# A 700-word memset on GpSimd in front of every indirect DMA, known to the schedule

## The chip, the core and the metric

The kernel runs on one core of a Trainium2 chip. What is measured is the device time of one execution in microseconds (us). The engines go by the names of the profile: PE is TensorE (PEld its weight loads), DVE is VectorE, ACT is ScalarE, POOL is GpSimd and SP is SyncE, which issues the plain DMAs. An *indirect* DMA (rows picked by a list of indices) is issued by POOL.

## The reference

A Fourier transform along the sequence, a complex linear layer with soft thresholding, the transform back, and then a mixture of 8 experts in which every expert takes exactly 2496 of the 19968 tokens, by a greedy assignment in the order of the logits:

```python
X = np.fft.rfft(x, axis=1)                       # x: 8 x 2496 x 256
Yr = Xr @ w_r - Xi @ w_i + b_r
Yi = Xr @ w_i + Xi @ w_r + b_i
Yr = np.sign(Yr) * np.maximum(np.abs(Yr) - lam, 0.0)   # Yi likewise
y = np.fft.irfft(Y, n=x.shape[1], axis=1)
...
logits = x @ w_gate                              # x = y as 19968 x 256, 8 experts
order = np.argsort(-flat)
for idx in order:                                # token, expert
    if assigned[tok] >= 0 or counts[e] >= cap: continue
    assigned[tok] = e; counts[e] += 1            # cap = 2496
...
for e in range(E):                               # w1[e]: 256 x 1024, w2[e]: 1024 x 256
    h = np.maximum(x[mask] @ w1[e], 0.0)
    out[mask] = h @ w2[e]
```

## The kernel before

The program has two parts that overlap a little. Up to about 640 us the transforms run as matrix products, batch by batch; in them POOL has elementwise work (L893 and L1116 write the low halves of numbers that are split in two for the matmuls). The transform's result goes to the DRAM tensor `YD`, one row of 256 words per token.

Then come the experts. Each has an *early* job of 512 tokens, whose lists are known before the last batches are transformed, and a *late* job of 1984 tokens, taken in an order that the routing decides. A late job of an expert consists of these steps, and each of the eight takes some 110 us:

- the router (DVE searches thresholds by counting, L419 and L423, with small matmuls L429 and L430; then a list of token numbers from matmuls L516, ACT's sign sums L521 and L522 and DVE),
- four gathers of the expert's weights by POOL (`Experts.load`, L578, buffers `raw`), split in two halves by ACT (L586) and DVE (L587),
- 16 gathers of 128 tokens each by POOL (L600), two into one buffer of the group `xg`,
- per chunk of 512 tokens (four gathers): eight transposes on PE (L615) into one PSUM bank (group `psx`, a single one), split by ACT (L618) and DVE (L619),
- the first layer on PE (L630), relu and split by ACT (L633) and DVE (L634),
- the second layer on PE (L646), 24 matmuls for 128 tokens, copied by ACT (L649) into one of the four buffers of the group `os` (in the profile xTh and xTl),
- 16 scatters of 128 tokens each by POOL (L653), each with a memset of a single word ahead of it (L652).

Names in the profile are those of the buffers, which the groups share: xg, xT and hid are names like yTl, s1st, z, FG and s2h.

No order is written out by hand. The class `Plan` takes all tasks with an engine, an assumed duration, a position and the tasks they depend on, simulates them, and at each step emits the task that can start first (the lowest position where several can). So the order of every engine's instructions follows from the assumed durations. An indirect DMA is such a task of POOL (`Kit.ind`, L309): 1.05 us of POOL, and a `load` that says when its data are there, by way of one queue for all DMAs:

```python
def ind(...): return self.plan.add('P', 1.05, pos, emit, reads, writes, load=moved(nbytes, run, 1.2, 1.4, late))
...
if t.load is not None:
    lead, work, back = t.load
    self.queue = max(self.queue, start + lead) + work
    t.end = self.queue + back
```

There are 352 indirect DMAs: 160 gathers and 160 scatters of tokens (32 of each in the early jobs) and 32 of weights. Once emitted, the order on an engine is fixed: each instruction waits for the semaphores of what it reads and for the instruction ahead of it.

Of the kernel before, what the change touches and what calls it, by code (L numbers as in the profile page):

```python
# [77 lines left out]
class Buf:  # L78

    def __init__(self, kind, alloc, state=False):  # L80
        self.state = state
        self.kind, self.alloc, self.t, self.got = kind, alloc, None, False
        self.writers, self.users = [], []
# [172 lines left out]
        return max(t.end for t in self.tasks)  # L256


LATE = dict(sp=2.0, raw=8.0, gather=2.0, scatter=3.0)
SLACK = dict(split=2.0, count=0.3, back=0.2, lists=0.5, os=0.3, hid=0.2)  # L260


def moved(nbytes, run, lead=1.6, back=1.8, late=0.0): return lead, nbytes / run * (0.009 + 3.68e-5 * run if run <= 4096 else 7e-5 * run) / 16, back + late
# [21 lines left out]
class Kit:  # L285
# [20 lines left out]

    def dma(self, pos, emit, nbytes, reads, writes, run=1024, late=0.0, **k): return self.plan.add('SP', 0.4, pos, emit, reads, writes, load=moved(nbytes, run, late=LATE['sp'] + late), **k)

    def ind(self, pos, emit, nbytes, reads, writes, run=1024, late=0.0): return self.plan.add('P', 1.05, pos, emit, reads, writes, load=moved(nbytes, run, 1.2, 1.4, late))  # L309


HALF = CAP / 2
# [242 lines left out]
class Experts:  # L555

    def __init__(self, K, H, YD, YDb, w1, w2, out):
        self.K, self.H, self.YD, self.YDb, self.out = K, H, YD, YDb, out
        self.w = (w1, w2)
        self.rows = (w1.rearrange("e d f -> (e d) f"), w2.rearrange("e (r m) d -> (e r) (m d)", m=4))  # L560
        self.spacer = K.one("spacer_b", [1, 1])
        self.scat = []

    def load(self, pos, e=None, wi=None):
# [3 lines left out]
        for k in range(2):  # L568
            for m in range(2):
# [7 lines left out]
                else:  # L577
                    K.ind(p, lambda r=r, k=k, m=m: K.P.indirect_dma_start(out=r.t, out_offset=None, in_=self.rows[k],  # L578
                                                                          in_offset=bass.IndirectOffsetOnAxis(ap=wi.t[:, m:m + 1], axis=0)), 524e3, [wi], [r], run=4096, late=LATE['raw'])

# [9 lines left out]
    def run(self, n, base, W, gi, go, gs, oi, oo, pos_g, early=False):  # L590

        K, H, plan, v = self.K, self.H, self.K.plan, self.K.v
        V, A, P, T = K.V, K.A, K.P, K.T
# [3 lines left out]
        for t in range(NT):  # L597
            if not t % 2: xg[t // 2] = K.sb("xg", [128, 2, 256])
            g = xg[t // 2]
            q = K.ind(pos_g(t), lambda t=t, g=g: P.indirect_dma_start(  # L600
                out=g.t[:, t % 2], out_offset=None, in_=self.YD[0:EB * S] if early else self.YD, in_offset=bass.IndirectOffsetOnAxis(ap=gi.t[:, go + t:go + t + 1], axis=0)),
                131e3, [gs[t]] + (self.YDb[0:EB] if early else self.YDb), [g], late=LATE['gather'])
            gi.users.append(q)
# [32 lines left out]
        def ffn2(c, q, pos):  # L636
            t = 4 * c + q
            M = min(128, n - 128 * t)
            ps, o = K.psum("pso", [128, 256]), K.sb("os", [128, 256])
            for qr in range(4):  # L640
                def mm(qr=qr):
                    k = 6 * qr
                    for ft in range(2 * qr, 2 * qr + 2):
                        hh, hl = hT[c, ft]
                        for a, w_ in ((hh, 0), (hh, 1), (hl, 0)):
                            T.matmul(ps.t[0:M], lhsT=a.t[:, 128 * q:128 * q + M], rhs=W2[ft // 4].t[:, w_, ft % 4], start=k == 0, stop=k == 23)  # L646
                            k += 1
                K.t(.708, pos + .5 * qr, mm, [W2[qr // 2]] + [x for ft in range(2 * qr, 2 * qr + 2) for x in hT[c, ft]], [ps], slack=SLACK['hid'])
            plan.add('A', .27, pos + 1, lambda: A.copy(o.t[0:M], ps.t[0:M]), [ps], [o], slack=SLACK['os'])  # L649

            def sc():
                P.memset(self.spacer.t, 0.0)  # L652
                ins = P.indirect_dma_start(out=self.out, out_offset=bass.IndirectOffsetOnAxis(ap=oi.t[0:M, oo + t:oo + t + 1], axis=0), in_=o.t[0:M], in_offset=None, bounds_check=N - 1, oob_is_err=False)  # L653
                for other in self.scat:
                    K.tc.declare_no_dep(ins.ins, other.ins, reason="distinct rows")
                self.scat.append(ins)
            K.ind(pos + 2, sc, 131e3, [o, oi], [], late=LATE['scatter'])

# [198 lines left out]
def phase_a(K, H, x, w_r, w_i, b_r, b_i, w_gate, cD1, cF, cG, cD5, YD, LG, NB=B):  # L857
# [25 lines left out]
    def add_dma(pos, emit, nbytes, reads=(), writes=(), eng='SP', after=(), run=1024):  # L883
        return plan.add(eng, 1.05 if eng == 'P' else 0.4, pos, emit, reads, writes, after=after, load=moved(nbytes, run, *((1.2, 1.4) if eng == 'P' else ()), late=LATE['sp']))

# [509 lines left out]
```

## Time and profile before

| | us |
|---|---|
| median of 3 runs (lowest to highest) | 1677.47 (1677.03 to 1680.85) |
| the profiled execution, whole | 1685.89 |
| its span, first to last instruction | 1684.0 |
| PE busy | 1569.3 (93%) |
| DVE busy | 1110.5 (66%) |
| ACT busy | 822.6 (49%) |
| POOL busy | 585.3 (35%) |
| mean granted clock of TensorE | 0.971 |

Times of the profile are microseconds from the span's start. A matmul's line gives the engine PE, the line of the kernel, the tile written and the tiles read. The granted clock is a share of TensorE's full speed: 1.00 is 2.4 GHz, 0.50 is 1.2 GHz. "Idle before" is the time in which the engine had nothing before that instruction, and behind the arrow stands what released it.

### The profile page before, as it was taken

The page shows a single profiled execution, that of the slowest core. Times are in us where ns is not written, and L with a number is a line of the kernel's source. Part 1 is how long each engine was busy: PE and PEld are TensorE (multiplying, and loading weights), DVE is VectorE, ACT ScalarE, POOL GpSimd, SP SyncE. Part 2 cuts the span into 40 slices and gives each one's busy share as a digit, 9 for nine tenths or more (in the row PEclk, how much of TensorE's full clock was granted, in tenths as well). Part 3 has the DMA queues.
Part 4 walks back from the last instruction along what each step waited for, and adds up shares of the span by engine and source line. Part 5 has one row for each costly group of instructions (what it writes and reads, how often), then busy time and mean ns, then how long its engine had stood idle before and what let it go on. Part 6 is the DMA issues. An engine that isn't in the chain of part 4 may idle for free.

```text
span 1684.0 us, 30703 instructions
## 1 busy us (share of the span) xinstructions
PE 1569.3 (93%) x10808; PEld 1379.7 (82%) x10808; DVE 1110.5 (66%) x3561; ACT 822.6 (49%) x1795; POOL 585.3 (35%) x711
## 2 busy tenths in 40 slices
PE   6999999999999989998998998997988989988997
PEld 3899999998888758986787887886878868867997
DVE  2666667668988855898788887785757645442321
ACT  1557767676687654445334343342433534542331
POOL 1014334343365553124326234233251242452121
PEclk7999999999999999999999999998999999989999
DMA  8777877877688554333112022121221111221000
GB/s 237 219 238 244 230 232 223 241 239 218 203 240 260 177 165 144 100 108 106 42 51 88 25 76 62 51 67 46 70 61 37 65 56 60 93 86 41 21 26 26
DMA packets 140071, 209.30 MB, mean 124 GB/s; under 512 B 31135, under 2 KB 102511, under 8 KB 139713
## 3 DMA queue, kind: packets, MB, share of 16 engines
q1 hardware_dynamic: 118612, 145.53, 28.8%
q0 software_dynamic: 21296, 61.73, 11.8%
q8 instruction: 87, 1.43, 0.4%
q14 instruction: 76, 0.62, 0.1%
HBM read 122.44 MB, written 84.75 MB: 123 GB/s over the span
## 4 chain that ended last, share of the span: by engine, by line
PE 68%; DVE 10%; issue 10%; ACT 3%; another core or an unknown queue 3%; POOL 3%; DMA 2%; SPq 0%; POOLq 0%; ACTq 0%; DVEq 0%
PE ps L646 19%; PE ps L630 12%; PE ps L1038 12%; PE p L630 6%; PE ps L1019 4%; PE ps L1052 4%; PE p L1086 3%; PE p L988 3%; POOL out_dram L653 2%; PE pt L1106 2%; PE ps L615 2%; DVE junk L419 1%; PE ps L1127 1%; DMA sh<-in_x_dram 1%
## 5 line engine op out<-in xcount | busy, mean ns | idle before, releaser
L1038 PE MATMUL ps<-wt,xTh 128*128 128x256 f32 x1280 | 245.5, 291 | 0.0
L1038 PEld LDWEIGHTS ps<-wt,xTh 128*128 128x128 f32 x1280 | 201.2, 190 | 5.4 <-issue 0.2
L1038 PE MATMUL ps<-wt,xTl 128*128 128x256 f32 x640 | 179.8, 281 | 0.7 <-DVE xTl L1029 0.7
L1116 POOL TENSOR_TENSOR yTl<-yr,yTh 128x468 bf16<-128x468 f32 (+1 forms) x88 | 97.9, 1113 | 173.4 <-ACT yTh L1113 128.9
L419 DVE SCALAR_TENSOR_TENSOR junk<-h_m,st,h_AG 128x156 bf16<-128x156 f32 (+1 forms) x472 | 155.4, 374 | 2.5
L653 POOL DMA_INDIRECT out_dram<-xTh,li x64 | 67.0, 1047 | 257.6 <-ACT xTh L649 244.3
L893 POOL TENSOR_TENSOR s2l<-s2c,s2h 120x512 fp32r<-120x512 f32 (+1 forms) x84 | 102.3, 1222 | 134.8 <-ACT s2h L890 131.3
L1038 PEld LDWEIGHTS ps<-wt,xTl 128*128 128x128 f32 x640 | 121.8, 190 | 0.9 <-DVE xTl L1029 0.9
L649 ACT COPY xTl<-ps 128x256 f32<-128x256 f32 x80 | 29.8, 373 | 169.5 <-PE ps L646 132.3
L649 ACT COPY xTh<-ps 128x256 f32<-128x256 f32 x80 | 29.9, 374 | 164.1 <-PE ps L646 122.3
L1019 PE MATMUL ps<-FG,sh 128*128 128x128 f32 x640 | 97.2, 283 | 7.3 <-DMA sh<-T 7.3
L1019 PEld LDWEIGHTS ps<-FG,sh 128*128 128x128 f32 x640 | 87.8, 194 | 15.8 <-issue 10.5
L653 POOL DMA_INDIRECT out_dram<-xTl,li x64 | 65.4, 1023 | 97.3 <-ACT xTl L649 82.6
L1029 DVE TENSOR_TENSOR xTl<-ps,xTh 128x512 fp32r<-128x512 f32 x80 | 54.9, 687 | 59.4 <-ACT xTh L1028 58.2
L1052 PE MATMUL ps<-z,FG 128*128 128x256 f32 x320 | 84.1, 385 | 3.4 <-DMA FG<-cG 1.1
L578 POOL DMA_INDIRECT xt<-in_moe_w_dram,wi x32 | 35.6, 1114 | 130.9 <-DVE h_certs L800 23.8
L1044 DVE TENSOR_TENSOR ps<-ps,bt 128x512 f32<-128x512 f32 x80 | 55.6, 694 | 32.4 <-PE ps L1038 29.3
L893 DVE TENSOR_TENSOR xl<-xt,xh 117x512 fp32r<-117x512 f32 (+1 forms) x77 | 61.6, 806 | 21.8 <-ACT xh L890 21.4
L1028 ACT CAST xTh<-ps 128x512 fp32r<-128x512 f32 x80 | 47.2, 590 | 49.4 <-PE ps L1019 43.8
L1111 DVE TENSOR_TENSOR yr<-pt,yTh 128x468 f32<-128x468 f32 (+1 forms) x77 | 48.1, 625 | 28.8 <-ACT yTh L1110 21.5
L646 PE MATMUL ps<-sh,yTh 128*128 128x256 f32 (+1 forms) x320 | 64.6, 284 | 2.4 <-ACT xTl L649 2.4
L1086 PE MATMUL p<-s2h,d 120*117 120x512 f32 (+1 forms) x168 | 66.6, 403 | 0.0
(722 smaller groups left out, 5097.8 us busy)
## 6 DMA issues: line engine op xcount, KB each, us to landing
sh<-T SPq DMA_DIRECT2D x40, 512.0 KB
T<-s4st SPq DMA_DIRECT2D x80, 256.0 KB
s2c<-T SPq DMA_DIRECT2D x80, 240.0 KB
YD<-yst SPq DMA_DIRECT2D x80, 234.0 KB
T<-s1st SPq DMA_DIRECT2D x73, 240.0 KB
xt<-in_moe_w_dram SPq DMA_DIRECT2D x32, 512.0 KB
xt<-in_x_dram SPq DMA_DIRECT2D x105, 156.0 KB
LG<-lgst SPq DMA_DIRECT2D x80, 21.9 KB
```

The lines of the kernel that those rows point to most:

```text
L419: v(cols + 59, p, lambda k=k: V.scalar_tensor_tensor(junk[k % 2].t[:, 0:cols], H.m[:, 0:cols], c.t[:, k // ng:k // ng + 1], ag(k % ng)[:, ...
L630: T.matmul(ps.t[:, 0:w], lhsT=W1[m].t[:, a, 128 * ft:128 * ft + 128], rhs=x_.t[:, 0:w], start=q + m == 0, stop=q + m == 3)
L646: T.matmul(ps.t[0:M], lhsT=a.t[:, 128 * q:128 * q + M], rhs=W2[ft // 4].t[:, w_, ft % 4], start=k == 0, stop=k == 23)
L649: plan.add('A', .27, pos + 1, lambda: A.copy(o.t[0:M], ps.t[0:M]), [ps], [o], slack=SLACK['os'])
L653: ins = P.indirect_dma_start(out=self.out, out_offset=bass.IndirectOffsetOnAxis(ap=oi.t[0:M, oo + t:oo + t + 1], axis=0), in_=o.t[0:M], in ...
L893: lambda: eng.tensor_tensor(lb[1](), src(), hb[1](), op=OP.subtract), [srcb, hb[0]], [lb[0]])
L1019: T.matmul(ps.t[:, i, 128 * dt:128 * dt + 128], lhsT=sh[k // 8].t[:, k % 8, 128 * dt:128 * dt + 128], rhs=at(Ft, k), start=True, stop=True)
L1038: T.matmul(ps3.t[:, i], lhsT=a.t[:, i, dt, o:o + 128], rhs=wt[c].t[:, w, dt], start=n == 0, stop=n == 11)
L1044: plan.add('V', dve(512), pos + 1.282, lambda ps3=ps3: V.tensor_tensor(ps3.t, ps3.t, bt[:, None, :].to_broadcast([128, 2, 256]), op=OP.add ...
L1052: T.matmul(ps4.t[:, i], lhsT=at(Gt, 2 * p + i), rhs=z.t[:, i], start=True, stop=True)
L1086: T.matmul(ps.t[0:M, gs_], lhsT=d5[0:k_, a, 0:M], rhs=v.t[0:k_, gs_], start=i == 0, stop=i == 2)
L1116: yq.append(plan.add('P', pool(2 * W), pos + 0.376, lambda yh=yh, yl=yl, yr=yr, W=W: P.tensor_tensor(yl.t[:, :, 0:W], yr.t[:, :, 0:W], yh. ...
```

## The change

Every indirect DMA is now issued right behind a memset of 700 words in one partition on POOL, into a buffer `gap` that nobody reads. The task in the plan gets longer by 0.982 us (0.1 + 1.26e-3 x 700), on POOL and in the lead of its data. The one-word memsets ahead of the scatters are gone.

```diff
+GAP = 700
...
-    def ind(self, pos, emit, nbytes, reads, writes, run=1024, late=0.0): return self.plan.add('P', 1.05, pos, emit, reads, writes, load=moved(nbytes, run, 1.2, 1.4, late))
+    def ind(self, pos, emit, nbytes, reads, writes, run=1024, late=0.0):
+        g = 0.1 + 1.26e-3 * GAP
+
+        def spaced():
+            self.P.memset(self.gap, 0.0)
+            return emit()
+        return self.plan.add('P', g + 1.05, pos, spaced, reads, writes, load=moved(nbytes, run, g + 1.2, 1.4, late))
...
-        self.spacer = K.one("spacer_b", [1, 1])
+        K.gap = K.one("gap", [1, GAP]).t
...
             def sc():
-                P.memset(self.spacer.t, 0.0)
                 ins = P.indirect_dma_start(out=self.out, ...
```

The memset has no operand in common with the DMA behind it, so it waits for nothing but POOL itself. Since the plan's durations change, so does the order on all engines; the same instructions are emitted otherwise. The lines of the new kernel are 6 or 7 higher (L600 is L607, L615 is L622, L630 is L637, L646 is L653, and the scatter L653 is L659; the memset is L314).

On POOL, at the late job of the fifth expert (the one whose gathers begin at 1229.62 us in the trace before): the tiles gathered are yTl, s1st, z, FG, s2h, two gathers each, and the scatters, from xTh and xTl, belong to the expert ahead of it. Before:

```order
467 L600 DMA yTl_16590<-YD,li_16584 128x256 x2
468 L600 DMA s1st_16621<-YD,li_16584 128x256 x2
469 L600 DMA z_16660<-YD,li_16584 128x256 x2
470 L652 MEMSET spacer_b 1x1
471 L653 DMA out_dram<-xTh_16681,li_15463 19968x256
472 L652 MEMSET spacer_b 1x1
473 L653 DMA out_dram<-xTl_16724,li_15463 19968x256
474 L600 DMA FG_16818<-YD,li_16584 128x256
475 L652 MEMSET spacer_b 1x1
476 L653 DMA out_dram<-xTh_16820,li_15463 19968x256
```

On POOL at the same job, now (the gathered tiles are FG and s2l):

```order
617 L314 MEMSET gap 1x700
618 L607 DMA FG_16704<-YD,li_16698 128x256
619 L314 MEMSET gap 1x700
620 L607 DMA FG_16704<-YD,li_16698 128x256
621 L314 MEMSET gap 1x700
622 L607 DMA s2l_16761<-YD,li_16698 128x256
623 L314 MEMSET gap 1x700
624 L607 DMA s2l_16761<-YD,li_16698 128x256
625 L314 MEMSET gap 1x700
626 L659 DMA out_dram<-xTh_16784,li_15544 19968x256
627 L314 MEMSET gap 1x700
628 L659 DMA out_dram<-xTl_16843,li_15544 19968x256
```

Six gathers in one run have become four with a memset ahead of each, and the scatters of the expert ahead stand right behind those four.

On PE at the same job before: the transposes (operand h_idn) of the first chunk write ps_16719 and ps_16753, those of the second chunk ps_16932; ps_16726 is a tile of the second layer of the expert ahead.

```order
6588 L615 MATMUL ps_16719<-h_idn,yTl_16590 128x128 x2
6589 L615 MATMUL ps_16719<-h_idn,s1st_16621 128x128 x2
6590 L646 MATMUL ps_16726<-FG_15083,s1st_16306 128x256 x2
...
6602 L615 MATMUL ps_16753<-h_idn,yTl_16590 128x128 x2
6603 L615 MATMUL ps_16753<-h_idn,s1st_16621 128x128 x2
6604 L630 MATMUL p_16761<-s2h_16733,sp_16202 128x512
...
6663 L630 MATMUL ps_16910<-yTl_16768,sp_16224 128x512
6664 L615 MATMUL ps_16932<-h_idn,z_16660 128x128 x2
6665 L615 MATMUL ps_16932<-h_idn,FG_16818 128x128 x2
```

On PE at the same job now: ps_16899 and ps_16963 take the first chunk's transposes, ps_17124 the second's, and ps_17099 is a tile of this expert's own second layer.

```order
6615 L622 MATMUL ps_16899<-h_idn,FG_16704 128x128 x2
6616 L622 MATMUL ps_16899<-h_idn,s2l_16761 128x128 x2
...
6629 L622 MATMUL ps_16963<-h_idn,FG_16704 128x128 x2
6630 L622 MATMUL ps_16963<-h_idn,s2l_16761 128x128 x2
6631 L637 MATMUL ps_16968<-s4st_16917,sp_16329 128x512
...
6694 L653 MATMUL ps_17099<-sh_16578,z_17046 128x256
6695 L622 MATMUL ps_17124<-h_idn,s2h_16960 128x128 x2
6696 L622 MATMUL ps_17124<-h_idn,yst_17019 128x128 x2
```

The second chunk's transposes have moved from behind 30 matmuls of the first layer (L630) to behind all 48 of that chunk and 12 of its second layer, and the second layer of the expert ahead is nearly done where the first transposes stand.

## Rows read from the trace of the kernel before

**Rows 1.** The profile page: busy time of each engine over the whole span (with its share of the span and its instructions), the granted clock of TensorE in 40 slices of 42.1 us (tenths of full speed), and the share of the span that each engine has in the chain of work that ended last.

```profile
PE 1569.3 (93%) x10808; PEld 1379.7 (82%) x10808; DVE 1110.5 (66%) x3561; ACT 822.6 (49%) x1795; POOL 585.3 (35%) x711
PEclk7999999999999999999999999998999999989999
PE 68%; DVE 10%; issue 10%; ACT 3%; another core or an unknown queue 3%; POOL 3%; DMA 2%; SPq 0%; POOLq 0%; ACTq 0%; DVEq 0%
```

**Rows 2.** Busy time by stretch of the span, for seven stretches of the late experts. Columns: from and to in us, length; then busy us (and instructions) of PE, PEld, DVE, ACT and POOL; the mean granted clock of TensorE; the mean busy share of the DMA engines; GB/s.

```profile
780.00:820.00 40.00, 33.54 (x220) 28.79 (x219) 29.89 (x127) 16.52 (x36) 21.73 (x26) 0.96 0.31 91
880.00:920.00 40.00, 35.12 (x218) 30.06 (x217) 32.17 (x130) 20.76 (x54) 25.80 (x27) 0.96 0.29 90
1020.00:1060.00 40.00, 34.61 (x217) 29.43 (x217) 31.30 (x157) 12.09 (x30) 16.07 (x22) 0.96 0.17 52
1120.00:1160.00 40.00, 29.93 (x184) 25.86 (x183) 22.72 (x105) 12.63 (x39) 19.84 (x25) 0.87 0.22 65
1220.00:1280.00 60.00, 48.04 (x307) 42.39 (x307) 36.37 (x170) 21.02 (x60) 23.04 (x30) 0.91 0.17 50
1340.00:1400.00 60.00, 51.95 (x330) 45.07 (x329) 29.61 (x134) 20.08 (x57) 24.11 (x32) 0.94 0.18 53
1460.00:1540.00 80.00, 63.99 (x378) 54.34 (x377) 31.18 (x76) 33.95 (x94) 42.20 (x51) 0.89 0.25 77
```

**Rows 3.** The same view for the seven stretches that lie between those (820 to 880, 920 to 1020, 1060 to 1120, 1160 to 1220, 1280 to 1340, 1400 to 1460 and 1540 to 1660 us; in each of them the granted clock is 1.00): the row with their sum.

```profile
sum 520.00, PE 513.83 PEld 463.08 DVE 336.92 ACT 199.46 POOL 133.62; mean PE 73.40 PEld 66.15 DVE 48.13 ACT 28.49 POOL 19.09
```

**Rows 4.** POOL in time order, three gathers of the expert that begins about 1230 us and a scatter that stands behind its one-word memset. Columns: start in us, duration in us, engine, line, operation, operands, and in brackets how long the engine was idle just before and what ended that; "issue" means that it waited for nothing the profile shows.

```profile
1229.62 0.99 POOL L600 DMA_INDIRECT yTl<-YD,li  x1 [5.00 <-PE ps L630]
1230.91 1.04 POOL L600 DMA_INDIRECT yTl<-YD,li  x1 [0.30 <-issue]
...
1249.98 1.01 POOL L653 DMA_INDIRECT out_dram<-xTh,li  x1 [0.22 <-issue]
...
1262.64 0.94 POOL L600 DMA_INDIRECT s1st<-YD,li  x1 [0.30 <-issue]
```

**Rows 5.** ACT in time order in the same stretch. "remote" is a release whose source the profile doesn't name.

```profile
1238.30 0.37 ACT L649 COPY xTh<-ps 128x256 f32<-128x256 f32 x1 [5.83 <-PE ps L646]
...
1263.05 0.60 ACT L633 ACTIVATE yst<-ps 128x512 fp32r<-128x512 f32 x1 [5.10 <-remote]
1265.90 0.59 ACT L618 CAST yTl<-ps 128x512 fp32r<-128x512 f32 x1 [2.25 <-remote]
```

**Rows 6.** PE in time order in the same stretch.

```profile
1233.65 0.28 PE L646 MATMUL ps<-FG,s4st 128*128 128x256 f32 x1
1240.19 0.55 PE L516 MATMUL p<-RDd,sh 128*128 128x157 f16 x3 [3.17 <-ACT jl L522]
1240.54 0.63 PE L615 MATMUL ps<-h_idn,yTl 128*128 128x128 f32 x2
...
1267.27 0.69 PE L615 MATMUL ps<-h_idn,z 128*128 128x128 f32 x2 [7.57 <-DVE s1st L619]
```

**Rows 7.** Some 70 us earlier, scatters that follow one another with time between them: the last matmul of a tile on PE, the copies of it and of the next tile's on ACT, and the two scatters on POOL. Columns as before.

```profile
1165.06 0.28 PE L646 MATMUL ps<-FG,yst 128*128 128x256 f32 x1
1165.37 0.37 ACT L649 COPY xTh<-ps 128x256 f32<-128x256 f32 x1 [2.23 <-PE pt L430]
1166.03 1.02 POOL L653 DMA_INDIRECT out_dram<-xTh,li  x1 [17.38 <-ACT xTh L649]
1169.04 1.01 POOL L653 DMA_INDIRECT out_dram<-xTl,li  x1 [1.92 <-ACT xTl L649]
```

**Rows 8.** POOL and ACT about 915 us: two gathers of one run that lie further apart than the others, and the ACT instruction that starts between them.

```profile
915.19 1.96 POOL L600 DMA_INDIRECT yr<-YD,li  x1 [0.30 <-issue]
917.45 0.95 POOL L600 DMA_INDIRECT yr<-YD,li  x1 [0.30 <-issue]
917.25 0.59 ACT L618 CAST s4st<-ps 128x512 fp32r<-128x512 f32 x1 [1.74 <-PE pt L430]
```

**Rows 9.** POOL's instructions by line and shape. Columns: line, engine, operation, operands, shapes, count; busy us and mean ns of one; idle us of the engine just before them, and what ended it. First the two that only write, then the largest elementwise operation.

```profile
L652 POOL MEMSET spacer_b<- 1x1 f32 x160 | 14.8, 92 | 0.0
masks.py:197 POOL MEMSET h_idn<- 128x128 f32 x1 | 0.3, 265 | 0.0
L1116 POOL TENSOR_TENSOR yTl<-yr,yTh 128x468 bf16<-128x468 f32 x80 | 89.7, 1121 | 141.6 <-ACT yTh L1113 97.1 <-DVE yTh L1115 13.3 <-PE p L988 12.4
```

**Rows 10.** The same for POOL's indirect DMAs from 640 us on: the 64 scatters that leave from buffers xTl (every second scatter of the late experts), and the weight gathers.

```profile
L653 POOL DMA_INDIRECT out_dram<-xTl,li x64 | 65.4, 1023 | 97.3 <-ACT xTl L649 82.6 <-DVE junk L419 5.6 <-issue 3.0
L578 POOL DMA_INDIRECT xt<-in_moe_w_dram,wi x32 | 35.6, 1114 | 130.9 <-DVE h_certs L800 23.8 <-DVE wi L830 23.6 <-DVE sp L587 20.7
```

**Rows 11.** Busy time by stretch again (columns as in rows 2), for the stretch in which the first experts' early jobs run beside the last of the transform.

```profile
500.00:600.00 100.00, 91.04 (x706) 78.22 (x704) 80.94 (x172) 69.28 (x173) 54.97 (x52) 0.97 0.68 209
```

**Rows 12.** POOL in time order, the last scatter of the program.

```profile
1674.53 0.91 POOL L653 DMA_INDIRECT out_dram<-xTl,li  x1 [1.73 <-ACT xTl L649]
```

**Rows 13.** VectorE beside POOL: a line of small tensor_scalars and a line of casts, each with its shortest, median and longest duration in ns and the first and last start; then one POOL operation and the VectorE cast that starts inside it, in time order.

```profile
L423 DVE TENSOR_SCALAR cnt<-acc x110: 149/170/1234, 409.6 to 1406.7; 128x4 bf16<-128x4 f32 x50, 128x9 bf16<-128x9 f32 x22, 128x6 bf16<-128x6 f32 x22, 128x3 bf16<-128x3 f32 x13
L1115 DVE CAST yTh<-yr x11: 404/405/924, 604.5 to 628.8; 128x468 bf16<-128x468 f32 x10, 128x312 bf16<-128x312 f32 x1
...
606.55 1.08 POOL L1116 TENSOR_TENSOR yTl<-yr,yTh 128x468 bf16<-128x468 f32 x1 [0.43 <-DVE yTh L1115]
606.97 0.92 DVE L1115 CAST yTh<-yr 128x468 bf16<-128x468 f32 x1
```

## The prediction

> **What bounds the kernel now.** I began with the page. PE is busy for 93% of the span and makes up 68% of the chain that ended last [rows 1], so only PE's lost time, or a lower clock, can be won back. The clock is at full speed (nine tenths or more) in nearly every slice, so the loss sits in short stretches. The view by stretch finds them: one at the change from each late expert to the next. In the seven stretches of [rows 2], 360 us together, PE is idle for 6.46 + 4.88 + 5.39 + 10.07 + 11.96 + 8.05 + 16.01 = 62.8 us, and the clock is below 1.00; length times the missing clock gives 1.6 + 1.6 + 1.6 + 5.2 + 5.4 + 3.6 + 8.8 = 27.8 us. Together 90.6 us. In the 520 us between them PE is idle for only 6.17 us at the full clock [rows 3], 1.2%. At that rate the 360 us would lose 4.3 us, so the changes of expert cost 86 us more than the work between them.
>
> Next I asked what happens in one such stretch. About 1230 us POOL issues the next expert's gathers, the first two 1.29 us apart, each waiting for nothing [rows 4]. The tile whose last matmul on PE ran from 1233.65 to 1233.93 [rows 6] is copied by ACT only at 1238.30, though ACT had been idle for 5.83 us and the profile puts that wait down to this PE work [rows 5]. So the news that PE is done arrives 4.4 us late. At 1263.05 ACT again ends a wait, of 5.10 us, put down to nothing on this core ("remote"), and another at 1265.90 [rows 5], 3.3 us after the last gather of that run began at 1262.64, and 2.3 after it ended [rows 4]. PE itself then waits: 3.17 us for the list matmuls (for ACT) and 7.57 us for the transposes (for DVE's split, itself late) [rows 6]. These two make 10.7 of the 11.96 us of idle in that stretch.
>
> With other spacing the delay isn't there. Two scatters at 1166.03 and 1169.04, 3.0 us apart, follow copies on ACT; the first copy starts at 1165.37, 0.03 us after its matmul ended (1165.06 + 0.28) [rows 7]. And about 915 us, where one gather of a run took 1.96 us, so that the next began 2.26 us after it, ACT's wait ended at 917.25, just ahead of that next gather [rows 8]. I read this so: while POOL issues gathers 1.3 us apart, PE's completion signals are held up for several us; with 2.3 us or more between them they get through. This is inference from times; the profile has no row for it.
>
> **What a memset of 700 words costs on POOL.** The trace has none. One word takes 92 ns; 128 words in each of 128 partitions take 265 ns [rows 9]. That is 173 ns for 127 words, 1.36 ns each, so 700 words take 92 + 699 x 1.36 = 1040 ns. The lower bound is 265 ns, if length hardly matters; the upper is the subtraction's rate, 1121 ns for 468 words [rows 9], 1.68 us for 700. I take 1.04, the only rate from two memsets. A DMA starts 0.22 us behind its memset, and the gathers of [rows 4] take 0.94 to 1.04 us, 0.99 on average; so the pitch of gathers grows from 1.29 to 1.04 + 0.22 + 0.99 = 2.25 us (1.48 to 2.89 by the bounds), practically the 2.26 us at which a signal got through.
>
> **The sum.** Gain: the 86 us at the changes of expert. I take 0.8 of it, -69 us: nine tenths of the idle time in the stretch looked at goes back to late signals, and the clock term counts some idle time twice. The ends are 0 and -86.
>
> Costs. *Four gathers before the first transposes:* the fourth is 3 x (2.25 - 1.29) = 2.9 us later. Now 10.9 us lie between the first gather (1229.62 [rows 4]) and the first transposes (1240.54 [rows 6]), filled by the expert ahead's second layer; the new order puts still more of that layer there, and the second chunk's transposes behind the whole first layer of the first. If that cover is gone, 2.9 us per expert are exposed, 23 us in all. I take +4.
>
> *Scatters:* POOL is idle for 97.3/64 = 1.52 us ahead of every second one [rows 10], more than the 1.04 us of memset, which waits for nothing and runs in that time. Behind the four gathers scatters wait up to 4 us longer, ACT's copies then wait for one of four buffers, and PE for its two PSUM tiles. I take +4 (0 to 15: 2 us per expert).
>
> *Weight gathers:* 130.9/32 = 4.1 us idle ahead of each [rows 10]; the memset lies in it. 0.
>
> *Early jobs:* their 32 gathers add 32 x 0.96 = 31 us to POOL where it is 55% busy and PE 91% [rows 11]; half of that exposed is 15, and since POOL has the room I take +4 (0 to 15).
>
> *End of the program:* the last scatter has 1.73 us idle ahead of it [rows 12], which hides its memset. 0.
>
> *VectorE held by the memsets:* a cast that takes 0.40 us took 0.92 when it started inside POOL's subtraction (606.55 to 607.63, the cast from 606.97 to 607.89), and one of the 110 small tensor_scalars took 1.23 us instead of 0.17 [rows 13]. So POOL's elementwise work can hold DVE; whether a memset in one partition does, no row shows. 352 memsets of 1.04 us are 366 us, 0.31 of the span from 500 us on. If each of the 110 that meets one were held for half of it, DVE would lose 110 x 0.31 x 0.52 = 18 us, for a whole one 35. DVE is busy for 336.92 of 520 us there [rows 3] and makes up 10% of the chain [rows 1], so I take +3 (0 to 35).
>
> The Trainium skill, page "SBUF — State Buffer", section "Who interferes with whom", says that copies, casts and tensor_scalars of VectorE can use the port pair shared with GpSimd, and that whichever is first keeps it for its whole instruction while the other is fully blocked. The two long instructions of [rows 13] agree; by this rule the memsets would block too, and the sum would be -54 + 15 = -39 with the half (1638 us) and -22 with the whole (1655 us).
>
> Together -69 + 4 + 4 + 4 + 3 = -54. The span of 1684.0 becomes 1630, the profiled execution 1685.89 becomes 1632; the median of the runs lies 8.4 below the profiled execution, so I predict 1677.5 - 54 = 1623 us.
>
> **The rivals.**
> *Half the delay stays* (some signals still late at 2.25 us): -43 + 15 = -28, 1649 us. For it: 2.25 is just at the spacing seen to work, and that once.
> *The memsets hold VectorE:* 35 in place of 3, 1623 + 32 = 1655 us. For it: [rows 13]; against it: the POOL operation there reads and writes 128 partitions, the memset writes one.
> *The memset is short* (0.27 us): the pitch is 1.48 us, the signals stay late, the new order alone moves little, 1675 us. Against it: a length that costs nothing would be odd next to 2.4 ns a word in the subtraction.
> *Slower: the wider spacing doesn't let signals through but stretches the hold.* The release at 1265.90 came 3.3 us after the last gather began, more than the new pitch of 2.25. If quiet of that length is needed, every run of gathers is now one longer hold: 2.25/1.29 = 1.74 times, so the 86 us become 150, +64 + 15 = +79, 1756 us. It decides from the point where a quarter of the runs behave so in full and nothing is won in the others: 0.25 x 64 + 15 = +31, 1708 us. Against it: [rows 8].
>
> **How the numbers follow.** Chances: the forecast 0.60, half of it 0.18, VectorE held 0.08, short memset 0.05, slower 0.09. The predicted time is the first one's. Its own range reaches from all of the excess won at no cost (1677.5 - 86 = 1591) to the half case, 1649. The range on record, 1590 to 1672, takes in the cases of half and of VectorE; the short memset and the slower case, 0.14, lie outside. Within 0.3% (5 us) is about what a measurement of this kernel cannot tell from no change: 0.05 (the short memset). Faster: 0.60 + 0.18 + 0.08 = 0.86. Slower: 0.09.
>
> **What would show it.** Right: rows of `gap` at about 1.04 us, gathers 2.25 us apart, ACT's copies of [rows 5] starting within 0.1 us of their matmul, no "remote" waits of several us, PE's waits of 3 and 7.6 us gone, and in stretches like [rows 2] PE above 95% at a clock near 1.00. Wrong: memsets far from 1.04 us; the 4 to 6 us waits still there, or longer, in each run of gathers; the transposes waiting for gather data, or PE for scatters' buffers; the tensor_scalars of [rows 13] with a median well above 170 ns.

## The result and the profile after

The changed kernel takes 1630.38 us (median of 4 runs, 1626.18 to 1632.67) beside 1678.22 us for the kernel before (4 runs): a ratio of 0.971, with a 95% interval of 0.9685 to 0.9735. The prediction was 1623 us. Later the same two kernels were compared again on two other occasions, where the kernel before took 1607 and 1606 us and the changed one 1626 and 1627; that is the main finding of the experiments and comes below. An *occasion* is a set of runs taken side by side, the kernel before always among them.

The page of the changed kernel's profile (answering to [rows 1]): busy time, granted clock, chain, and the group of the new memsets.

```profile
PE 1546.8 (95%) x10808; PEld 1366.0 (84%) x10808; DVE 1127.4 (69%) x3561; ACT 826.2 (51%) x1795; POOL 808.8 (50%) x903
PEclk7999999999999999999999999999999999999999
PE 70%; DVE 14%; issue 7%; POOL 3%; ACT 3%; DMA 2%; SPq 0%; POOLq 0%; DVEq 0%; ACTq 0%
L314 POOL MEMSET gap<- 1x700 f32 x352 | 237.2, 674 | 0.1
```

Four things are to be seen. PE does the same 10808 matmuls in 22.5 us less busy time. After the first slice no slice has a clock below nine tenths. A memset of 700 words takes 0.67 us, not 1.04. And DVE, which does the same 3561 instructions, is busy 17 us longer and has a larger part of the chain.

The stretches of the changed kernel that hold the changes of expert (answering to [rows 2], same columns):

```profile
780.00:820.00 40.00, 38.77 (x273) 34.07 (x272) 37.22 (x167) 20.48 (x49) 33.15 (x38) 1.00 0.26 85
880.00:920.00 40.00, 37.39 (x258) 33.82 (x258) 36.74 (x155) 18.30 (x42) 31.71 (x39) 1.00 0.25 83
1000.00:1040.00 40.00, 38.94 (x261) 34.15 (x260) 36.80 (x179) 16.66 (x47) 30.73 (x38) 1.00 0.20 59
1100.00:1140.00 40.00, 38.30 (x257) 33.61 (x256) 32.54 (x154) 17.29 (x51) 30.51 (x38) 1.00 0.20 62
1200.00:1240.00 40.00, 37.56 (x253) 32.95 (x252) 32.83 (x150) 16.67 (x50) 29.68 (x36) 1.00 0.18 55
1300.00:1360.00 60.00, 54.69 (x353) 48.42 (x352) 37.74 (x143) 23.90 (x65) 39.74 (x48) 0.94 0.17 53
1420.00:1480.00 60.00, 54.85 (x344) 46.89 (x343) 33.11 (x76) 29.86 (x78) 48.00 (x58) 0.97 0.26 83
```

PE is idle for 19.5 of these 320 us and the clock takes 60 x 0.06 + 60 x 0.03 = 5.4 us more: 24.9 us, where the same sum was 90.6 before. The 440 us between them (820 to 1540 us) lose 6.7 us, 1.5%. So the changes of expert now cost 20 us more than the work between them, and cost 86 before: 66 us are won.

The gathers of the fifth late expert on POOL now (answering to [rows 4]):

```profile
1203.71 0.99 POOL L607 DMA_INDIRECT FG<-YD,li  x1 [4.25 <-PE p L637]
1204.69 0.67 POOL L314 MEMSET gap<- 1x700 f32 x1
1205.53 0.97 POOL L607 DMA_INDIRECT FG<-YD,li  x1 [0.16 <-issue]
1206.50 0.67 POOL L314 MEMSET gap<- 1x700 f32 x1
1207.34 0.95 POOL L607 DMA_INDIRECT s2l<-YD,li  x1 [0.16 <-issue]
```

They lie 1.82 and 1.81 us apart. In the midst of them, on PE and ACT (answering to [rows 5, 6]), the last matmul of a tile and its copy:

```profile
1207.64 0.28 PE L653 MATMUL ps<-FG,z 128*128 128x256 f32 x1
...
1207.95 0.37 ACT L656 COPY xTh<-ps 128x256 f32<-128x256 f32 x1 [1.36 <-PE ps L653]
```

The matmul ends at 1207.92 and ACT starts 0.03 us later; before, such a copy came 4.4 us late.

The same can be counted over the whole late part, from 640 us on. Which matmul an ACT instruction waited for is read from a trace of the same order in which no signal was late (the experiments below give one for each of the two orders), since a held signal is easily put down to a later matmul. A signal is called late if ACT began more than 0.5 us after both that matmul's end and the end of its own instruction ahead: 28 of 385 waits for PE in the kernel before (the worst 6.5 us, all of them together 85.9 us of ACT's time), none of 412 in the changed one. Of the 28, 22 had two or more of POOL's DMAs started in the 2.4 us ahead of the matmul's end, and 6 had one; of the 176 waits with none, no signal was late. VectorE's waits for PE show it too, 5 of 44 late before (the worst 4.9 us) and none now. The counts of late signals below are those of ACT.

### The profile page after: what moved, and what is told of

The parts are those of the page before. It is cut to its first block, busy times and chain, and to the rows that moved or that the text cites. A ratio compares the mean times of both kernels' runs of the same rounds, so it can differ in the third digit from the quotient of the medians.

```text
span 1624.1 us, 30932 instructions
## 1 busy us (share of the span) xinstructions
PE 1546.8 (95%) x10808; PEld 1366.0 (84%) x10808; DVE 1127.4 (69%) x3561; ACT 826.2 (51%) x1795; POOL 808.8 (50%) x903
## 4 chain that ended last, share of the span: by engine, by line
PE 70%; DVE 14%; issue 7%; POOL 3%; ACT 3%; DMA 2%; SPq 0%; POOLq 0%; DVEq 0%; ACTq 0%
PE ps L653 21%; PE ps L637 13%; PE ps L1044 11%; PE p L637 6%; PE ps L1025 4%; PE ps L1058 4%; PE p L994 3%; PE p L1092 3%; DVE junk L426 2%; PE ps L622 2%; PE pt L1112 2%; POOL out_dram L659 1%; POOL gap L314 1%; DMA sh<-in_x_dram 1%; DVE sh L594 1%
## 5 line engine op out<-in xcount | busy, mean ns | idle before, releaser
L314 POOL MEMSET gap<- 1x700 f32 x352 | 237.2, 674 | 0.1
L659 POOL DMA_INDIRECT out_dram<-xTh,li x64 | 65.1, 1018 | 133.0 <-ACT xTh L656 129.3
L659 POOL DMA_INDIRECT out_dram<-xTl,li x64 | 66.1, 1032 | 53.8 <-ACT xTl L656 43.9
L1117 DVE TENSOR_TENSOR yr<-pt,yTh 128x468 f32<-128x468 f32 (+1 forms) x77 | 48.2, 626 | 30.1 <-ACT yTh L1116 22.5
```

The source lines that it names most:

```text
L314: self.P.memset(self.gap, 0.0)
```

## The experiments

There are two theories. A: the time between POOL's gathers decides whether PE's completion signals get through. B: the gain comes from the new order on the engines. Memsets of one word keep the new order and take the time away; memsets that the plan doesn't count keep the time and the old order.

**The order without the time.**

```diff
-            self.P.memset(self.gap, 0.0)
+            self.P.memset(self.gap[:, 0:1], 0.0)
```

> The order of the changed kernel on every engine, instruction for instruction, but each memset writes 1 word instead of 700, so two gathers of a run are again about 1.3 us apart. Theory A (the time between gathers on POOL lets PE's completion signals through): the waits of 4 to 6 us on ACT in the runs of gathers come back, and most of the gain is lost: 1660 to 1690 us. Theory B (the gain comes from the order, with the gathers earlier or later against PE's work): about 1630 us, as with the memsets.

Measured: 1645.3 us (1642.48 to 1650.81) beside 1691.0 for the kernel before on that occasion, ratio 0.9723 (0.9652 to 0.9793). Neither theory alone: the order by itself wins 46 us. The late signals are back, but fewer and shorter than before (21 of 398, the worst 3.8 us; ACT's delays add up to 34.7 us instead of 85.9). One of them, rows of POOL, PE and ACT in this kernel:

```profile
1229.62 0.95 POOL L607 DMA_INDIRECT yTl<-YD,li  x1 [0.21 <-issue]
...
1230.88 0.94 POOL L607 DMA_INDIRECT yTl<-YD,li  x1 [0.22 <-DVE junk L426]
```

```profile
1229.31 0.40 PE L637 MATMUL p<-yTh,sp 128*128 128x512 f32 x1
```

```profile
1233.50 0.60 ACT L640 ACTIVATE yTl<-p 128x512 fp32r<-128x512 f32 x1 [4.55 <-PE ps L637]
```

The matmuls into the tile end at 1229.71, the last gathers of the run start at 1229.62 and 1230.88, and ACT starts at 1233.50. So the new order has such delays too, but fewer and shorter ones. Why it meets fewer was not tested.

**The time without the order.**

```diff
-        g = 0.1 + 1.26e-3 * GAP
+        g = 0.0
```

> The memsets of 700 words in front of every indirect DMA, but the plan doesn't count them, so PE, DVE and ACT have the order of the kernel before, and POOL too except for the memsets. Theory A: the waits of several us go and most of the gain is there: 1625 to 1645 us. Theory B: no gain, and the gathers later than the order assumes: 1678 to 1700 us.

Measured: 1622.07 us (1620.19 to 1624.57) beside 1691.0, ratio 0.9576 (0.9508 to 0.9644), and no late signal (0 of 398). Theory A holds: the memsets alone, in the order of before (but for one swapped pair of PE's 10808 matmuls), win 69 us. The new order isn't needed for the gain.

**Which memsets, and how long.** In the changed kernel's order, memsets of 700 words ahead of the token gathers alone, and memsets of 350 words everywhere:

```diff
-            self.P.memset(self.gap, 0.0)
+            self.P.memset(self.gap if late == LATE['gather'] else self.gap[:, 0:1], 0.0)
```

> The order of the changed kernel; 700 words only in front of the token gathers (160), 1 word in front of scatters and weight gathers. Theory A: only runs of gathers held signals, so the time stays within 5 us of the changed kernel's 1630, or is a few us better, since scatters leave 0.6 us earlier. If runs of scatters or weight gathers hold signals as well at their 1.3 us pitch, some of the gain is lost: 1640 to 1655 us.

Measured: 1623.49 us beside 1691.0, ratio 0.9579 (0.9512 to 0.9647), 3 late signals of 411 (the worst 1.4 us). Memsets ahead of the gathers are enough, as theory A says. Whether those ahead of the other DMAs alone would do was not tested on an occasion on which signals were late.

```diff
-            self.P.memset(self.gap, 0.0)
+            self.P.memset(self.gap[:, 0:350], 0.0)
```

> The order of the changed kernel; every memset writes 350 words, by 92 ns + 0.83 ns a word 0.38 us, so a pitch of gathers of about 1.58 us instead of 1.8. Theory A with a gradual effect of the pitch: about half the gain, 1645 to 1660 us. With a threshold below 1.58 us: 1625 to 1632 us, all of it. With a threshold between 1.58 and 1.8 us: 1660 to 1690 us, as with one word. Theory B: 1630 us.

Measured: 1625.8 us, ratio 0.9601 (0.9533 to 0.9669), a pitch of 1.49 to 1.54 us in the runs of gathers and 10 late signals of 407 (the worst 3.0 us, 12.9 us added up). In this order 1.5 us is nearly enough.

**The kernel before takes 1607 us on another occasion.** The next four were meant to refine theory A.

> The changed kernel itself (one empty line more), for the comparison with the others on one chip. Both theories: as before, 0.971 of the kernel before.

Measured: 1626.19 us (1624.64 to 1628.77), but the kernel before beside it took 1607.11 us: ratio 1.0125 (1.0108 to 1.0142). The expectation failed in the half that I hadn't questioned: the changed kernel was the same, the kernel before 71 to 84 us faster than on the two occasions ahead.

```diff
-        g = 0.1 + 1.26e-3 * GAP
+        g = 0.0
...
-            self.P.memset(self.gap, 0.0)
+            self.P.memset(self.gap if late == LATE['gather'] else self.gap[:, 0:1], 0.0)
```

> The order of the kernel before; 700 words in front of the 160 token gathers alone, 1 word in front of scatters and weight gathers, and the plan counts none. Theory A: the runs of gathers are where signals were held, so this has the gain of the variant with all memsets in the old order (1622 us beside 1691 on that chip, ratio 0.958), to within 5 us. Theory B (the memsets ahead of scatters and weight gathers matter as well): 10 to 30 us slower than that variant.

Measured: 1616.55 us, ratio 1.0066 (1.005 to 1.0083) to the kernel before.

```diff
-            self.P.memset(self.gap, 0.0)
+            gather = late == LATE['gather']
+            self.turn = gather and not getattr(self, 'turn', False)
+            if not gather or self.turn: self.P.memset(self.gap, 0.0)
+            if self.turn: self.P.memset(self.gap, 0.0)
```

(with g = 0.0 too)

> The order of the kernel before and as much memset time as with 700 words in front of every indirect DMA, but token gathers come in pairs: two memsets of 700 words ahead of the first of a pair, none ahead of the second, so pitches of about 1.3 and 2.4 us in turn. Theory A with the pitch of each neighbour deciding: part of the signals are held again, for at most about 2.5 us each: 20 to 40 us slower than with even spacing. Theory A2 (the mean pitch decides, POOL's DMA rate averaged over several gathers): the same as even spacing, within 5 us.

Measured: 1633.93 us, ratio 1.0174 (1.0156 to 1.0193), and no late signal in spite of pitches of 1.3 us. It can't tell neighbours from the mean, since on this occasion no signal was held anywhere.

```diff
-            self.P.memset(self.gap, 0.0)
+            self.P.memset(self.gap[:, 0:1] if late == LATE['gather'] else self.gap, 0.0)
```

> The order of the changed kernel; 700 words in front of scatters and weight gathers, 1 word in front of the token gathers, so these are 1.3 us apart again. Theory A: like the variant with one word everywhere in this order (1645 us beside 1691, ratio 0.972), within 8 us. Theory B (any memset among POOL's DMAs will do): like the changed kernel.

Measured: 1620.78 us, ratio 1.008 (1.006 to 1.0101). It has runs of gathers 1.25 us apart, as the kernel with one word everywhere had, and none of its 409 waits is late, 76 of them with two DMAs or more close ahead. So the delay itself was missing on this occasion, which none of the theories had foreseen. I formed theory C: the hold belongs to the occasion, and where it is absent the change only costs.

**The kernel before, with a profile, on a further occasion.**

> The kernel before (one comment line more), with a profile on this chip. Its time has been 1678, 1691 and 1607 us on three occasions, while the changed kernel stayed at 1626 to 1630. Theory C (whether PE's signals are held in runs of gathers 1.25 us apart depends on the chip or the placement a run gets; the change costs some 19 us where they are not held): either about 1607 us with ACT's copies starting within 0.1 us of their matmuls inside the runs of gathers, or 1675 to 1695 us with waits of 2 to 6 us there. Rival D (the whole chip was faster that time, signals held or not): a time near 1607 us with such waits in the trace, or near 1680 without.

Measured: 1606.41 us (10 runs, 1604.03 to 1608.45), with 0 late signals of 393. Its gathers of the fifth late expert, and the work around them (POOL, PE and ACT), show the same burst as [rows 4]:

```profile
1197.12 0.99 POOL L600 DMA_INDIRECT yTl<-YD,li  x1 [5.00 <-PE ps L630]
1198.41 1.03 POOL L600 DMA_INDIRECT yTl<-YD,li  x1 [0.30 <-issue]
...
1203.63 0.95 POOL L600 DMA_INDIRECT z<-YD,li  x1 [0.30 <-issue]
```

```profile
1201.14 0.28 PE L646 MATMUL ps<-FG,s4st 128*128 128x256 f32 x1
...
1204.57 0.38 PE L615 MATMUL ps<-h_idn,yTl 128*128 128x128 f32 x2
```

```profile
1201.45 0.37 ACT L649 COPY xTh<-ps 128x256 f32<-128x256 f32 x1 [1.49 <-PE ps L646]
```

Six gathers in one run at 1.3 us, and the copy still starts 0.03 us after its matmul; the transposes follow 7.5 us after the first gather instead of 10.9. In the seven stretches with the changes of expert PE now does this (their sum, columns by name):

```profile
sum 300.00, PE 294.04 PEld 262.28 DVE 230.68 ACT 141.96 POOL 185.25; mean PE 42.01 PEld 37.47 DVE 32.95 ACT 20.28 POOL 26.46
```

6.0 us idle, and the clock is below 1.00 in one stretch only (0.97 for 60 us, 1.8 us). Less the 1.3% of the stretches between them, the changes of expert cost 4 us here, against 86 on the first occasion. Rival D is out: the time and the late signals go together.

> The changed kernel on the same chip. Theory C: 1622 to 1632 us wherever it runs, with no late signals, so 1.2% slower than the kernel before if that stands at 1607 us, and 3 to 4% faster if that stands at 1675 to 1695 us. Rival D: it moves with the kernel before, ratio 0.97.

Measured: 1626.83 us (1625.86 to 1627.75) beside 1605.81, ratio 1.0137 (1.012 to 1.0154), as theory C says. The waits of PE in its trace agree with those of the first occasion's changed kernel to 0.1 us in the longest ones (4.2, 2.4 and 2.0 us in both).

> The order of the kernel before, 350 words in front of the token gathers alone (pitch about 1.5 us), 1 word in front of the other indirect DMAs; the plan counts none. Theory C: on a chip that doesn't hold signals about 1611 us (half of the 9.5 us that 700 words cost in this order), on one that does 1615 to 1630 us, since 350 words left only 9 of 433 signals freshly late in the other order. Against it: if 1.5 us is too short in the longer runs of this order, 1635 us or more.

```diff
-        g = 0.1 + 1.26e-3 * GAP
+        g = 0.0
...
-            self.P.memset(self.gap, 0.0)
+            self.P.memset(self.gap[:, 0:350] if late == LATE['gather'] else self.gap[:, 0:1], 0.0)
```

Measured: 1606.97 us beside 1605.81, ratio 1.0004 (0.9994 to 1.0013). Spacing the gathers to 1.5 us in the old order costs nothing that can be measured, less than the 5 us expected.

**The last run: the same kernel once more.**

> The same kernel as gathers_half_old_order, in the hope of an occasion on which signals are held (the kernel before at 1677 us or more beside it). Theory C there: 1615 to 1635 us, since 350 words in the other order left 1626 us; if 1.5 us is too short in this order's longer runs of gathers, 1640 to 1665 us. On an occasion without holds it repeats 1607 us, level with the kernel before, and tells nothing new.

Measured: 1636.45 us (1635.62 to 1640.38) beside 1693.73, ratio 0.9645 (0.9601 to 0.9689). The hold was back, and the same kernel file that had taken 1607 us took 1636. It has 35 late signals of 393, 58.0 us added up, so part of the hold stays; the time lies between the range expected for enough spacing and the one for too little. Two things come together here. In a run of gathers with steps of 1.5 us alone (1015.04 to 1022.61) a signal is 2.4 us late (the matmul ends at 1020.76, ACT starts at 1023.20), so 1.5 us isn't enough in this order's long runs. And the scatters and weight gathers have one word ahead of them, which puts steps of 1.3 us into the runs; there the worst signal is 6.0 us late. POOL there, and the copy of a tile whose last matmul ends at 901.55:

```profile
899.40 0.96 POOL L607 DMA_INDIRECT yTl<-YD,li  x1 [0.16 <-issue]
900.67 1.03 POOL L659 DMA_INDIRECT out_dram<-xTh,li  x1 [0.22 <-issue]
902.21 0.97 POOL L607 DMA_INDIRECT yst<-YD,li  x1 [0.16 <-issue]
903.49 1.02 POOL L659 DMA_INDIRECT out_dram<-xTl,li  x1 [0.22 <-issue]
```

```profile
907.57 0.37 ACT L656 COPY xTh<-ps 128x256 f32<-128x256 f32 x1 [7.03 <-PE ps L653]
```

**What marks the two kinds of occasion.** The kernel before stood at 1678, 1691 and 1694 us on three occasions (the first, the second and the fifth) and at 1607 and 1606 on two (the third and the fourth); within each it kept its level (1685 to 1705 over 7 runs on the second, 1603 to 1608 over 19 on the fourth). The profile itself marks the difference. In the view of DMA issues, the kernel before on the first occasion has no time from issue to landing for POOL's indirect DMAs:

```profile
out_dram<-xTh,li POOLq DMA_INDIRECT x64
...
xt<-in_moe_w_dram,wi POOLq DMA_INDIRECT x32
```

and the same kernel on the fourth has (last number, us):

```profile
out_dram<-xTh,li POOLq DMA_INDIRECT x64, 2.5
...
xt<-in_moe_w_dram,wi POOLq DMA_INDIRECT x32, 4.3
```

Behind it stand the records of semaphore updates. The eight semaphores that POOL's DMAs report to have 5857 of them in the trace on the fourth occasion and 3626 on the first, for the same program; the changed kernel has 5845 on the fourth and 4860 on the first. All seven traces in which the landing times are missing come from the three occasions on which the kernel before took 1678 us or more, all seven that have them from the other two. The engines' own signals are thinned out as well: for the 2732 DVE instructions that report to DVE's semaphore, the kernel before has 2525 records on the first occasion and 2733 on the fourth; for PE's 1712 it has 1672 and 1712. So on those three occasions semaphore updates are lost or merged in the record, and signals that should release an engine are late on the same occasions. Where nothing is held, PE's signals are prompt: in the two kernels of the third occasion with the old order (700 words ahead of the gathers alone, and gathers in pairs) all of them are recorded within 0.23 us of their matmul's end. The DMA transfers themselves are no slower: the packets took 41.1% of 1684 us on the first occasion and 43.0% of 1605 us on the fourth, 692 and 690 us.

What makes an occasion one or the other stays open. The kernel doesn't: the same file took 1607 and 1636 us. The chip's number doesn't either: the record has number 0 for the second and the fourth occasion and 15 for the third and the fifth, so each was on both kinds. Every run on record has a granted clock beside its time, so each was taken with the profiler on; whether signals are held without it is not shown.

## Why the prediction was right, and where it was not

**The bound and the mechanism.** Right on the occasion it was made for. The 86 us at the changes of expert were held signals: they fall to 4 us where nothing is held, and the profiled execution of the kernel before from 1685.9 to 1606.9. The copies start 0.03 us after their matmuls, and the waits of [rows 6] are gone, as the prediction's list asked; PE above 95% is reached in three of the seven stretches only, and a wait of 4.25 us stands there, where the kernel before without holds has none over 2.7. What it had wrong is whose 86 us they are: it took them for a property of the kernel, and they are one of the occasion. No rival had that. On two of the three occasions on which both kernels ran, the change makes the kernel 1.25 to 1.4% slower.

Two of the rows behind the mechanism showed less than was read from them. In [rows 7] POOL had issued nothing for 17 us when the first copy started, so that copy shows no hold without DMAs near it, not with DMAs 3 us apart. In [rows 8] the cast at 917.25 belongs to transposes that ended at 915.56: it was 1.7 us late, and the longer step only ended its hold. The reading held up all the same, by the experiments.

**The gain.** Predicted -69 (0.8 of 86); the excess fell by 66. But the fifth that remains isn't what the prediction meant: no signal is late any more, so 82 us of hold are gone, and 16 us of other losses have come at the same places, by the order and the memsets. That 69 and 66 lie so close is luck. In all the median fell by 48 us, where 54 were forecast.

**The memset.** Predicted 1040 ns, bounds 265 to 1680; measured 672, so (672 - 92)/699 = 0.83 ns a word. The slope was taken from a memset of 128 partitions: at 0.83 ns a word its 128 words would take 197 ns in one partition, and it took 265. The pitch came out at 1.8 us instead of 2.25. The gain didn't suffer, since 1.8 us is enough, where I had read 2.3 as the spacing that works: two errors that met, which is luck. The steps measured on the occasions with holds are 1.3 us (21 of 398 late in the new order, 28 of 385 in the old), 1.5 us (10 of 407, and 35 of 393 with steps of 1.3 us among them) and 1.8 us (0 of 412 and 0 of 398).

**The costs.** Predicted +15; the changed kernel is 19 and 21 us behind the kernel before on the two occasions without holds, where nothing else is in the difference. Part of it is early: PE's busy time in the stretch with the early jobs, kernel before and changed kernel on the fourth occasion,

```profile
500.00:640.00 140.00, 129.40 (x981) 106.85 (x980) 100.09 (x204) 90.35 (x215) 73.30 (x73) 0.96 0.67 198
```

```profile
500.00:640.00 140.00, 124.39 (x948) 101.70 (x947) 103.91 (x204) 89.63 (x213) 89.35 (x91) 0.98 0.64 193
```

is 5 us less, where the term was +4. Between 760 and 1540 us it is 13 us less (763.66 and 750.58 us); how that divides among the other terms was not measured. The memsets ahead of the gathers alone, in the old order, cost 9.4 us (1616.55 against 1607.11).

**VectorE held by the memsets.** The term was +3 for the time, with 18 us of DVE time if each small tensor_scalar that meets a memset is held for half of it. The mechanism was right, and the argument against it (a memset in one partition wouldn't) was wrong. In the changed kernel, VectorE and POOL in time order just ahead of the sixth expert's first layer:

```profile
1318.38 0.18 DVE L548 TENSOR_SCALAR li<-li 128x16 f32<-128x16 f32 x1
1318.59 0.26 DVE L545 TENSOR_SCALAR or<-li 128x16 f32<-128x16 f32 x1
1318.88 0.66 DVE L546 TENSOR_SCALAR or<-or 128x16 f32<-128x16 f32 x1
```

```profile
1318.84 0.67 POOL L314 MEMSET gap<- 1x700 f32 x1
```

and the line's shortest, median and longest duration, in the changed kernel on the first occasion and in the kernel before on the fourth:

```profile
L546 DVE TENSOR_SCALAR or<-or x24: 174/176/680, 798.0 to 1450.7; 128x16 f32<-128x16 f32 x24
```

```profile
L539 DVE TENSOR_SCALAR or<-or x24: 174/175/276, 793.1 to 1433.8; 128x16 f32<-128x16 f32 x24
```

The tensor_scalar that starts 0.04 us into the memset ends 0.03 us after it. Over the program 75 tensor_scalars start inside a 700-word memset and take 15.3 us more than their medians, 48 of them at least 0.05 us more; the 246 scalar_tensor_tensors that do so take 1.3 us more. This is what the Trainium skill, page "SBUF — State Buffer", section "Who interferes with whom", says: of the two engines the one that is first keeps the shared ports for its whole instruction, and tensor_scalar is among the operations that can want them. The trace agrees, with one partition of 700 words on GpSimd's side. That 15.3 us is near the 18 reckoned is luck: of the 110 instructions of the one line behind the 18 us (L430 now) 15 met a memset and lost 2.6 us, their median stayed at 172 ns, and the rest was lost in lines that the prediction left out. How much of the 15.3 us ends up in the time was not measured apart; the longest wait of PE in the late part,

```profile
1323.27 0.69 PE L622 MATMUL ps<-h_idn,s4st 128*128 128x128 f32 x2 [4.25 <-DVE s2h L626]
```

ends a chain on DVE in which two instructions (L546 twice) are held for 0.5 us each, but most of it is the list's arithmetic standing ahead of the split in the new order.

**The order.** The prediction didn't price it apart from the memsets, only as cover for the four gathers. It is worth 46 us by itself on an occasion with holds, and nothing can be seen of it beside the memsets (1622 us in the old order, 1623 in the new one with the gathers' memsets alone). The two gains are one and the same loss avoided twice, which a sum of terms can't show. The scatters' and weight gathers' terms (+4 and 0) were not measured apart. Side by side on the third occasion, in the old order, the kernel with memsets ahead of the scatters and weight gathers and double ones ahead of every second gather took 17 us more than the one with single memsets ahead of the gathers alone; which of the two differences costs it is open.

**A version that beats both** is not shown. The gathers spaced to 1.5 us in the old order are level with the kernel before where nothing is held (1607) and win 57 us where signals are held (1636 against 1694), but the changed kernel took 1630 on another occasion with holds. All memsets in the old order took 1622 on an occasion with holds and 700 words ahead of the gathers alone 1617 on one without; neither was run on the other kind.

## What to carry to other kernels

A profile is of one occasion: before a stall that no instruction explains is taken for the kernel's own, run the unchanged kernel again at another time, with its trace. Where an engine that has been idle starts microseconds after the matmul that it waited for, look at what POOL issues at that time; more time between its indirect DMAs is a cure that is worth what the occasion costs, and a price of its own where there is nothing to cure. A filler instruction on GpSimd isn't free on VectorE: a memset of one partition held most of the tensor_scalars that met it.

## What the runs showed that I had not expected

- The same program takes 1606 or 1694 us, 5% apart, each level steady within an occasion, by whether PE's completion signals are held up in runs of gathers 1.25 to 1.3 us apart.
- On the first occasion, with held signals, the trace of the kernel before has 3626 of the 5857 updates of the semaphores of POOL's DMAs, and no landing times for these DMAs; on the other two such occasions the landing times are missing as well.
- A memset in one partition on GpSimd takes 92 ns for one word, 381 for 350 and 672 for 700: 0.83 ns a word.
- It can hold VectorE's tensor_scalars to its end (0.66 us instead of 0.18), as the subtraction of [rows 13] held a cast.
